# A new hand-written order on TensorE, VectorE and ScalarE in a top-k attention and MLP kernel: pacing by estimated engine times, a PSUM bank for the values, a shorter weight conversion, loads in order of need

## The chip, the cores and the metric

The kernel runs on one core of a Trainium2 chip. The metric is the device time of one execution in microseconds (us). Engines are named as the profile names them: PE is TensorE (PEld its weight loads), DVE is VectorE, ACT is ScalarE, POOL is GpSimd, SP is SyncE, whose queue issues the DMAs here. All numbers are float32, apart from the two MLP weights, which arrive as float64.

## What is computed

Attention with a top-32 mask, and on its output an MLP with a smooth ReLU:

```python
B, H, S, D = 8, 8, 576, 64
scores = q @ k.T / sqrt(D)                     # per batch and head: 576 x 576
kth    = the 32nd largest score of each row
attn   = softmax(where(scores >= kth, scores, -1e9))
x      = (attn @ v) as (B*S, H*D) = 4608 x 512
h      = x @ w_in                              # 512 x 2048
g      = where(h >= 1, h, where(h <= -1, 0, (h + 1)**2 / 4))
out    = g @ w_out                             # 2048 x 512
```

## The kernel before, in words

**Steps.** Rows of queries are taken in tiles of 128 (four whole tiles and a tail of 64 rows per batch). One *step* is one tile of queries for one pair of heads: 144 steps, numbered m = 0 to 143, 18 per batch. A step consists of these parts, each in a function of its own:

- `scores` (before: line 209): four matmuls (L221) into four PSUM tiles `sp`, each evicted by ACT to `s` (L224).
- `weights` (L229): on DVE. The row's larger and smaller halves are formed (`more` L238, `less` L256), four rounds of MAX8 and MATCH_REPLACE8 (L244, L251) find the 32nd largest; ACT computes the exponentials `e` (L248) from the row maximum, which POOL negates (`nmax`, L246); DVE applies the mask and sums (L271), POOL multiplies by the reciprocal (L279).
- `transpose_w` (L283): PE transposes `e` into `pw` and `pwt` (L290, L293), and ACT copies them to `wT` and `wTt`.
- `values` (L297): PE multiplies with the values into `po` (L305, L313), and ACT copies to `xT` (L318, L320).

`keys_of` (L170) and `queries_of` (L196) load and transpose the keys of a batch and the queries of a tile (`pk`, `pkt`, `pq`).

**MLP.** Tiles of 128 tokens are gathered in chunks, mostly of two tiles. `mlp` (L329) turns a chunk into a list of small pieces. `hidden(f)` makes 128 of the 2048 hidden channels: four matmuls into `ph` (L336), then ACT writes `r` and `g` from `ph` (L340, L342), and POOL finishes `g` in three operations (L343 to L345); there are two buffers of `r`. `final` makes the output of one tile in `py` (L353), two of the sixteen `f` at a time; after the last, ACT copies `py` to `y` (L357), which a DMA stores. A hidden piece of a two-tile chunk and a final piece cost 8 units each, a hidden piece of one tile 4; there are 4608 units in all.

**Weights.** The float64 weights come as pairs of 32-bit words in 64 pieces of 128 x 256 values. `weight_piece` (L78) makes float32 of them with integer operations: three DVE operations (L85, L86, L90), two on ACT (L92, L97), two on POOL (L93, L94), and one more on DVE (L99). They are converted inside `weights`, through the calls of `between()`, one piece at each of six places in a step, from step 0 on; four pieces come ahead of step 0. A piece of MLP work is placed only where the weights that it needs have been converted earlier in the program.

**PSUM.** There are eight banks: four under the tag "a", taken in turn by `sp`, `pk`, `pkt`, `pq`, `pw`, `pwt` and `po`; three for `ph`; one for `py`.

**The order.** On PE and DVE the instructions stand as the program issues them (`manual_schedule`, L411). On ACT, POOL and SP a scheduler chooses the order when the program is built. The loop (L445) issues for step m: `values(m-2)`, `scores(m+1)`, `weights(m)`, a share of the waiting MLP pieces, `transpose_w(m-1)`, the queries and keys that come next, and another share. `advance` (L401) places pieces up to an even share of what is left over the steps that are left. A chunk's pieces become available two steps after its last step: the first chunk at m = 5, the second at m = 9, the third at m = 17.

**After the loop**, a check that the 32nd value was found rightly (`excess`, L264) is reduced to one flag (L478 to L483); were it set, the program would run again with a slower, exact search. With these inputs it is not set.

Of the kernel before, what the change touches and what calls it, by code (L numbers as in the profile page):

```python
# [22 lines left out]
def kernel(  # L23
# [34 lines left out]
    nc.gpsimd.memset(half, 0.5)  # L58
    minus = const.tile([P, 1], F32, name="minus")
    nc.gpsimd.memset(minus, -1.0)  # L60
    w_in = const.tile([P, NK, DFF], F32, name="w_in")
    w_out = const.tile([P, NF, DM], F32, name="w_out")

# [12 lines left out]
    WC = 256  # L76

    def weight_piece(pool, dst, src):  # L78
        raw = pool.tile([P, 2 * WC], U32, name="raw", bufs=2)
        nc.sync.dma_start(out=raw, in_=src.bitcast(U32))  # L80
        words = raw.rearrange("p (n t) -> p n t", t=2)
        lo, hi = words[:, :, 0], words[:, :, 1]

        top = pool.tile([P, WC], U32, name="top", bufs=2)
        nc.vector.tensor_scalar(top, hi, 3, 0x3FFFFFFF, ALU.logical_shift_left, ALU.bitwise_and)  # L85
        nc.vector.scalar_tensor_tensor(out=top, in0=hi, scalar=0xC0000000, in1=top,  # L86
                                       op0=ALU.bitwise_and, op1=ALU.bitwise_or)

        unit = pool.tile([P, WC], U32, name="unit", bufs=2)
        nc.vector.tensor_scalar(unit, top, 0xFF800000, None, ALU.bitwise_and)  # L90
        low = pool.tile([P, WC], F32, name="low", bufs=2)
        nc.scalar.activation(low, lo, AF.Copy, scale=2.0 ** -52)  # L92
        nc.gpsimd.tensor_tensor(out=low, in0=low, in1=unit.bitcast(F32), op=ALU.mult)  # L93
        nc.gpsimd.tensor_tensor(out=low, in0=low, in1=top.bitcast(F32), op=ALU.add)  # L94

        size = pool.tile([P, WC], F32, name="size", bufs=2)
        nc.scalar.activation(size, hi.bitcast(F32), AF.Abs)  # L97
        yield
        nc.vector.scalar_tensor_tensor(out=dst, in0=size, scalar=1.125 * 2.0 ** -15, in1=low,  # L99
                                       op0=ALU.is_ge, op1=ALU.mult)  # L100

    def weight_pieces(pool):
# [19 lines left out]
    def run(ctx, paired):  # L122
# [47 lines left out]
        def keys_of(b):  # L170

            kT = stage.tile([P, NHP, S], F32, name="kT")
            v_in, v_tl = load_values(b)
            k_tl = stage.tile([TL, H, D], F32, name="k_tl", bufs=1)
            nc.sync.dma_start(out=k_tl, in_=k[b, :, SM:S, :].rearrange("h p d -> p h d"))
            for hp in range(NHP):
                k_in = stage.tile([P, NT, 2, D], F32, name="k_in")
                for j in range(2):
                    nc.sync.dma_start(out=k_in[:, :, j, :], in_=whole(k, b)[:, 2 * hp + j])
                pt = ps.tile([P, NT, P], F32, name="pk", tag="a", bufs=4)  # L180
                for c in range(NT):
                    nc.tensor.transpose(pt[:, c, :], k_in[:, c].rearrange("p j d -> p (j d)"), ident)
                for j in range(2):
                    d = slice(j * D, (j + 1) * D)
                    nc.scalar.copy(kT[d, hp, main(j)], pt[d].rearrange("p c n -> p (c n)"))
                if hp == 0:
                    pt = ps.tile([P, NHP, TL], F32, name="pkt", tag="a", bufs=4)
                    for h2 in range(NHP):
                        nc.tensor.transpose(pt[:, h2, :], k_tl[:, 2 * h2:2 * h2 + 2].rearrange("p j d -> p (j d)"),
                                            ident[0:TL, 0:TL])  # L190
                    for j in range(2):
                        d = slice(j * D, (j + 1) * D)
                        nc.scalar.copy(kT[d, :, tail(j)], pt[d])
                yield dict(kT=kT, v=v_in, v_tl=v_tl)

        def queries_of(q_in, t):  # L196
            n = P if t < NT else TL
# [99 lines left out]
        def values(st):  # L297
            t, hp, v_in, v_tl = st["t"], st["hp"], st["keys"]["v"], st["keys"]["v_tl"]
            wT, wTt = st["wT"], st["wTt"]
            po = ps.tile([P, P], F32, name="po", tag="a", bufs=4)  # L300
            if t < NT:
                for c in range(NT + 1):
                    for j in range(2):
                        h = 2 * hp + j
                        nc.tensor.matmul(po[j * D:(j + 1) * D], v_in[:, h, c, :] if c < NT else v_tl[0][:, h, :],  # L305
                                         wT[:, j, c, :] if c < NT else wTt, start=(c == 0), stop=(c == NT))
            else:
                for i in range(2):
                    cols = slice(i * TL, (i + 1) * TL)
                    for c in range(NT + 1):  # L310
                        for j in range(2):
                            h = 2 * (hp + i) + j
                            nc.tensor.matmul(po[j * D:(j + 1) * D, cols], v_in[:, h, c, :] if c < NT else v_tl[1][:, h, :],  # L313
                                             wT[:, i, c, j * TL:(j + 1) * TL] if c < NT else wTt[:, j * TL:(j + 1) * TL],
                                             start=(c == 0), stop=(c == NT))
            xT, col = st["xT"]
            if t < NT:
                nc.scalar.copy(xT[:, hp, col:col + P], po)  # L318
            else:
                nc.scalar.copy(xT[:, hp:hp + 2, col:col + TL], po.rearrange("p (i n) -> p i n", i=2))  # L320
# [7 lines left out]

        def mlp(xT, tiles, pool):  # L329
            cw = len(tiles) * P  # L330
            gs = []

            def hidden(f):
                ph = ps.tile([P, CW], F32, name="ph", tag="ph", bufs=3)[:, 0:cw]
                for kk in range(NK):
                    nc.tensor.matmul(ph, w_in[:, kk, f * P:(f + 1) * P], xT[:, kk, 0:cw],  # L336
                                     start=(kk == 0), stop=(kk == NK - 1))
# [10 lines left out]
            def final(i, f0, f1, pys={}):  # L348
# [4 lines left out]
                    nc.tensor.matmul(py, gs[f][:, i * P:(i + 1) * P], w_out[:, f, :],  # L353
                                     start=(f == 0), stop=(f == NF - 1))
                if f1 == NF:
                    y = pool.tile([P, DM], F32, name="y", bufs=2)
                    nc.scalar.copy(y, py)  # L357
                    for p0, p1, rows in rows_of(*tiles[i]):
                        nc.sync.dma_start(out=rows, in_=y[p0:p1])
# [38 lines left out]
                converted += 1  # L398
                next(pieces_left)

        def advance(amount):  # L401
            nonlocal spent, due
            due += amount
            while pending and pending[0][1] <= converted and due >= pending[0][0]:
                cost, _, work = pending.popleft()
                due -= cost
                spent += cost
                work()
            due = min(due, 8.0)

        order = tc.manual_schedule(engines={mybir.EngineType.PE, mybir.EngineType.DVE})  # L411
        order.__enter__()
        keys, xTs = {}, {}
        q_ins, qTs = {}, {}
# [3 lines left out]
                q_ins[rounds[i]] = load_queries(*rounds[i])  # L418

        fetch(0)  # L420
        for got in keys_of(0):
            keys[0] = got
        fetch(1)
        prep = None
        state = []

        def queries(m):
            if m < n and steps[m][0:2] not in qTs:
                r = steps[m][0:2]
                qTs[r] = queries_of(q_ins[r], r[1])  # L430
                fetch(rounds.index(r) + 2)

        def begin(m):
            b, t, hp, ch, col = steps[m]
# [4 lines left out]

        queries(0)  # L440
        begin(0)
        for _ in range(4):
            convert()
        next_keys = 1
        for m in range(n + 2):  # L445
            if 2 <= m:
                values(state[m - 2])
                state[m - 2] = None
                for ch in [c for c in range(len(chunks)) if ready[c] == m - 2]:
                    pending.extend(mlp(xTs[ch], chunks[ch], mlp_pool))  # L450
            share = (total - spent) / (n + 2 - m)
            if m + 1 < n:
                begin(m + 1)
            if m < n:
                weights(state[m], convert)
            advance(share / 2)
            if 1 <= m <= n:
                transpose_w(state[m - 1])
            queries(m + 2)
            if m < n and prep is None and next_keys < B and steps[m][0] == next_keys - 1 and steps[m][1] >= 1:  # L460
                prep = keys_of(next_keys)
            if prep is not None and m % 2 == 0:
                got = next(prep, None)
                if got is None:
                    prep, next_keys = None, next_keys + 1
                else:
                    keys[next_keys] = got
            advance(share / 2)
        while pending:
            advance(8.0)  # L470
        order.__exit__(None, None, None)

    with ExitStack() as inner:
        run(inner, True)
    flag = const.tile([1, 8], I32, name="flag")
    with tc.tile_pool(name="end", bufs=1) as end, tc.tile_pool(name="endps", bufs=1, space=PSUM) as endps:
        worst = end.tile([P, 8], F32, name="worst")
        nc.vector.max(out=worst, in_=excess)  # L478
        pt = endps.tile([1, P], F32, name="pt")
        nc.tensor.transpose(pt, worst[:, 0:1], ident)  # L480
        top = end.tile([1, 8], F32, name="top8")
        nc.vector.max(out=top, in_=pt)
        nc.vector.tensor_scalar(flag, top, 0.0, None, ALU.is_gt)  # L483
    again = nc.values_load(flag[0:1, 0:1], min_val=0, max_val=1)
    with tc.If(again > 0):
        with ExitStack() as inner:
# [28 lines left out]
```

## Time and profile before

| what | us |
|---|---|
| median of 3 runs | 1920.29 (1918.97 to 1921.25) |
| the profiled execution | 1915.05, its span 1913.0 |
| first conversion of a weight piece on DVE starts | 18.28 |
| DVE starts step 0, step 1, step 10, step 17, step 143 | 30.56, 51.95, 252.18, 333.16, 1845.01 |
| last `py` matmul ends, and `y` is issued to be stored | 1904.7, 1905.36 |
| the five steps on DVE from 291.59 to 344.85, each | 10.3 to 11.7 |
| mean of one DVE conversion operation, L85, L86, L90, L99 | 0.377, 0.557, 0.367, 0.44 |
| mean of one POOL operation on 128 x 256 values, L93, L94 | 0.788, 0.836 |

How to read it: a step on DVE begins with `more` (L238), so the starts of that line are the clock of the kernel. In a group of instructions the first number is the busy time, the second the mean of one in ns, then the idle time of the engine just before them, with what ended it. The trace records each float32 matmul as two, so that a hidden piece of a two-tile chunk shows as 8 records of 128x256. A row of the timeline gives start, length, engine, line, operation, tiles, how many, and in brackets the idle time ahead of it.

### The profile page before, as it was taken

Reading aid. Unit: us, or ns where it says so; the run is one execution under the profiler, and the core shown is the slowest. Engines: PE = TensorE matmul, PEld = TensorE weight load, DVE = VectorE, ACT = ScalarE, POOL = GpSimd, SP = SyncE. Lnnn points to the kernel's source line nnn. Section 1 sums busy time; section 2 is a strip of 40 time slices with the busy share of each in tenths; the row PEclk is TensorE's granted clock in tenths of the full one; section 3 lists DMA queues with packets and bytes.
Section 4 is the critical chain, followed back from the end, with each engine's and each line's share of the span. In section 5 each row is a group of like instructions: output and inputs, shape, how many; then the busy total and the mean of one; then the engine's idle time right before and its main releaser. Section 6 shows DMA issues by size and latency. Waiting matters only on the chain.

```text
span 1913.0 us, 32251 instructions
## 1 busy us (share of the span) xinstructions
PE 1679.1 (88%) x10129; PEld 1160.1 (61%) x10129; DVE 1625.4 (85%) x5011; ACT 977.1 (51%) x2429; POOL 1028.8 (54%) x1772
## 2 busy tenths in 40 slices
PE   2346478898999999998999999998999999998998
PEld 1234255656676685767575776666676667666565
DVE  5998989999999799999898898989987879879640
ACT  4345455546455564655454655555455555445432
POOL 3567572725454672818283674637274554553553
PEclk8667679899999999999999999999999999998999
DMA  6222210011010000110010000110010000000000
GB/s 173 80 78 77 77 28 17 26 30 24 9 40 20 23 18 23 32 36 12 16 38 23 21 12 24 40 27 12 23 31 25 11 12 11 10 12 7 6 7 14
DMA packets 107445, 57.75 MB, mean 30 GB/s; under 512 B 86272, under 2 KB 94464, under 8 KB 107264
## 3 DMA queue, kind: packets, MB, share of 16 engines
q1 hardware_dynamic: 107264, 55.59, 10.6%
q8 instruction: 82, 1.34, 0.3%
q14 instruction: 99, 0.81, 0.1%
HBM read 46.14 MB, written 9.44 MB: 29 GB/s over the span
## 4 chain that ended last, share of the span: by engine, by line
PE 53%; DVE 22%; POOL 13%; ACT 6%; issue 5%; DMA 1%; POOLq 0%; SPq 0%; DVEq 0%; ACTq 0%
PE py L353 24%; PE ph L336 11%; PE sp L221 6%; DVE tops L244 6%; PE po L305 5%; DVE more L251 5%; PE pw L290 4%; POOL g L345 4%; POOL r L344 3%; POOL e L279 2%; POOL r L343 2%; DVE e L271 2%; DVE more L238 2%; DVE seconds L259 2%; DVE less L256 1%
## 5 line engine op out<-in xcount | busy, mean ns | idle before, releaser
L353 PE MATMUL py<-w_out,g 128*128 128x512 f32 x1152 | 534.7, 607 | 41.7 <-DVE w_out L99 37.1
L336 PE MATMUL ph<-xT,w_in 128*128 128x256 f32 (+1 forms) x2816 | 553.3, 353 | 3.9 <-ACT g L342 2.8
L336 PEld LDWEIGHTS ph<-xT,w_in 128*128 128x128 f32 x2816 | 466.4, 197 | 83.0 <-issue 29.4
L244 DVE MAX8 tops<-more 128x8 f32<-128x288 f32 x1152 | 468.5, 448 | 5.0
L353 PEld LDWEIGHTS py<-w_out,g 128*128 128x128 f32 x1152 | 209.2, 191 | 286.4 <-issue 219.8
L251 DVE MATCH_REPLACE8 more<-tops,more 128x288 f32<-128x288 f32 x864 | 375.9, 443 | 0.0
L279 POOL TENSOR_SCALAR e<-e,rz 128x576 f32<-128x576 f32 x288 | 242.4, 850 | 130.9 <-DVE rz L277 104.9
L340 ACT ACTIVATE r<-ph,half 128x256 f32<-128x256 f32 (+1 forms) x352 | 153.9, 437 | 264.2 <-POOL g L345 135.2
L264 POOL TENSOR_TENSOR excess<-seconds,kth 128x2 f32<-128x2 f32 x144 | 39.2, 273 | 417.3 <-DVE kth L263 416.4
L271 DVE SCALAR_TENSOR_TENSOR e<-s,kth,e 128x576 f32<-128x576 f32 x288 | 242.4, 875 | 23.1 <-ACT e L248 6.6
L345 POOL TENSOR_TENSOR g<-r,g 128x256 f32<-128x256 f32 (+1 forms) x352 | 246.7, 701 | 24.0
L291 ACT COPY wT<-pw 128x512 f32<-128x512 f32 x288 | 155.5, 594 | 202.3 <-PE pw L290 202.3
L290 PE MATMUL pw<-ident,e 128*128 128x128 f32 x1152 | 161.5, 284 | 110.6 <-POOL e L279 105.9
L248 ACT ACTIVATE e<-s,nmax 128x576 f32<-128x576 f32 x288 | 213.1, 786 | 75.2 <-POOL nmax L246 74.4
L238 DVE TENSOR_TENSOR more<-s 128x576 f32<-128x576 f32 x144 | 130.4, 905 | 139.0 <-ACT s L224 138.6
L344 POOL TENSOR_TENSOR r<-r 128x256 f32<-128x256 f32 (+1 forms) x352 | 230.4, 655 | 26.1
L290 PEld LDWEIGHTS pw<-ident,e 128*128 128x128 f32 x1152 | 138.0, 146 | 162.5 <-POOL e L279 118.2
L221 PE MATMUL sp<-kT,qT 64*128 64x288 f32 x1024 | 196.5, 442 | 34.7 <-ACT xT L318 26.4
L224 ACT ACTIVATE s<-sp 128x288 f32<-128x288 f32 x576 | 197.9, 417 | 40.7 <-PE sp L221 36.8
L343 POOL TENSOR_SCALAR r<-r 128x256 f32<-128x256 f32 (+1 forms) x352 | 155.4, 441 | 93.5 <-ACT r L340 93.2
L305 PEld LDWEIGHTS po<-wT,v_in 128*64 128x64 f32 x2048 | 118.0, 140 | 74.8 <-issue 40.0
L221 PEld LDWEIGHTS sp<-kT,qT 64*128 64x128 f32 x1024 | 109.1, 189 | 84.6 <-ACT xT L318 39.4
(61 smaller groups left out, 1592.7 us busy)
## 6 DMA issues: line engine op xcount, KB each, us to landing
q_in<-in_q_dram SPq DMA_DIRECT2D x32, 256.0 KB, 3.0
v_in<-in_v_dram SPq DMA_DIRECT2D x8, 1024.0 KB, 5.8
k_in<-in_k_dram SPq DMA_DIRECT2D x64, 128.0 KB, 3.0
raw<-in_moe_w_in_dram SPq DMA_DIRECT2D x32, 256.0 KB, 2.7
raw<-in_moe_w_out_dram SPq DMA_DIRECT2D x32, 256.0 KB, 2.8
out_dram<-y SPq DMA_DIRECT2D x32, 256.0 KB, 2.3
v_tail<-in_v_dram SPq DMA_DIRECT2D x16, 64.0 KB, 2.5
k_tl<-in_k_dram SPq DMA_DIRECT2D x8, 128.0 KB, 3.2
```

The lines of the kernel that those rows point to most:

```text
L221: nc.tensor.matmul(o[:, a0 - c0:a1 - c0], qT[d, g, :], kT[d, g, k0:k0 + a1 - a0], start=True, stop=True)
L244: nc.vector.max(out=tops[:, i, r:r + 8], in_=src[:, i, :])
L248: nc.scalar.activation(e[:, i, :], s[:, i, :], AF.Exp, bias=nmax[:, i:i + 1])
L251: nc.vector.match_replace(out=rest[:, i, :], in_to_replace=tops[:, i, r:r + 8], in_values=src[:, i, :], imm_value=LOWEST)
L271: nc.vector.scalar_tensor_tensor(out=e[:, i, :], in0=s[:, i, :], scalar=last[:, i:i + 1], in1=e[:, i, :], op0=ALU.is_ge, op1=ALU.mult, acc ...
L279: nc.gpsimd.tensor_scalar(e[:, i, :], e[:, i, :], rz[:, i:i + 1], 1.0, ALU.mult, ALU.mult)
L290: nc.tensor.transpose(pt[:, c, :], w[:, i, main(i)][:, c * P:(c + 1) * P], ident)
L305: nc.tensor.matmul(po[j * D:(j + 1) * D], v_in[:, h, c, :] if c < NT else v_tl[0][:, h, :], wT[:, j, c, :] if c < NT else wTt, start=(c == ...
L336: nc.tensor.matmul(ph, w_in[:, kk, f * P:(f + 1) * P], xT[:, kk, 0:cw], start=(kk == 0), stop=(kk == NK - 1))
L344: nc.gpsimd.tensor_tensor(out=r, in0=r, in1=r, op=ALU.mult)
L345: nc.gpsimd.tensor_tensor(out=g[:, 0:cw], in0=r, in1=g[:, 0:cw], op=ALU.add)
L353: nc.tensor.matmul(py, gs[f][:, i * P:(i + 1) * P], w_out[:, f, :], start=(f == 0), stop=(f == NF - 1))
```

## The change

It has six parts. (1) PE's pacing: `advance` gets a second way to place a piece, when a running estimate of PE's time (`pe_time`) lies before an estimate of DVE's (`done`), and is called three times in a step instead of two; queries and keys are placed ahead of `transpose_w`. (2) ACT's order is the program's, as PE's and DVE's are; in it the exponentials of step m stand ahead of the copies of `wT` of step m-1. (3) `po` gets a bank of its own. For that, two hidden pieces share one bank: `ph` is a tile of [128, 2, 256] with two buffers instead of [128, 256] with three. (4) A weight piece takes three DVE operations (L87, L96, L98 of the new file) instead of four, one on POOL (L91, an int32 add) instead of two, and 7 or 8 pieces are converted in a step, after 7 ahead of step 0. (5) The values of a batch are loaded after its keys, the tail of the keys after the first pair of heads, and `raw` has three buffers. (6) The check of `excess` is made inside the loop, at m = 144, ahead of the last chunk's MLP; `y` has one buffer.

```diff
     def weight_piece(pool, dst, src):
-        raw = pool.tile([P, 2 * WC], U32, name="raw", bufs=2)
+        raw = pool.tile([P, 2 * WC], U32, name="raw", bufs=3)
...
-        top = pool.tile([P, WC], U32, name="top", bufs=2)
-        nc.vector.tensor_scalar(top, hi, 3, 0x3FFFFFFF, ALU.logical_shift_left, ALU.bitwise_and)
-        nc.vector.scalar_tensor_tensor(out=top, in0=hi, scalar=0xC0000000, in1=top,
-                                       op0=ALU.bitwise_and, op1=ALU.bitwise_or)
-        unit = pool.tile([P, WC], U32, name="unit", bufs=2)
-        nc.vector.tensor_scalar(unit, top, 0xFF800000, None, ALU.bitwise_and)
-        low = pool.tile([P, WC], F32, name="low", bufs=2)
-        nc.scalar.activation(low, lo, AF.Copy, scale=2.0 ** -52)
-        nc.gpsimd.tensor_tensor(out=low, in0=low, in1=unit.bitcast(F32), op=ALU.mult)
-        nc.gpsimd.tensor_tensor(out=low, in0=low, in1=top.bitcast(F32), op=ALU.add)
+        bits = pool.tile([P, WC], U32, name="bits", bufs=2)
+        nc.vector.tensor_scalar(bits, hi, 3, None, ALU.logical_shift_left)
+        units = pool.tile([P, WC], F32, name="units", bufs=2)
+        nc.scalar.activation(units, lo, AF.Identity, bias=two, scale=2.0 ** -51)
+        nc.gpsimd.tensor_tensor(out=bits.bitcast(I32), in0=bits.bitcast(I32), in1=units.bitcast(I32), op=ALU.add)
         size = pool.tile([P, WC], F32, name="size", bufs=2)
         nc.scalar.activation(size, hi.bitcast(F32), AF.Abs)
         yield
-        nc.vector.scalar_tensor_tensor(out=dst, in0=size, scalar=1.125 * 2.0 ** -15, in1=low,
+        nc.vector.scalar_tensor_tensor(out=bits, in0=hi, scalar=0x80000000, in1=bits,
+                                       op0=ALU.bitwise_and, op1=ALU.bitwise_or)
+        nc.vector.scalar_tensor_tensor(out=dst, in0=size, scalar=1.125 * 2.0 ** -15, in1=bits.bitcast(F32),
                                        op0=ALU.is_ge, op1=ALU.mult)
...
         def values(st):
-            po = ps.tile([P, P], F32, name="po", tag="a", bufs=4)
+            po = ps.tile([P, P], F32, name="po", tag="po")
...
             def hidden(f):
-                ph = ps.tile([P, CW], F32, name="ph", tag="ph", bufs=3)[:, 0:cw]
+                if f % 2 == 0:
+                    phs.append(ps.tile([P, 2, CW], F32, name="ph", tag="ph", bufs=2))
+                ph = phs[-1][:, f % 2, 0:cw]
...
-        def advance(amount):
+        K_TIME, PIECE_TIME, UNIT_TIME = 10.2, 1.2, 0.22
+        pe_time, dve_time, done = 8.0, 10.0, {}
+
+        def advance(amount, until=0.0):
             due += amount
-            while pending and pending[0][1] <= converted and due >= pending[0][0]:
+            while pending and pending[0][1] <= converted and (due >= pending[0][0] or
+                                                              pe_time + pending[0][0] * UNIT_TIME < until):
                 cost, _, work = pending.popleft()
-                due -= cost
+                due = max(due - cost, 0.0)
                 spent += cost
+                pe_time += cost * UNIT_TIME
                 work()
...
-        order = tc.manual_schedule(engines={mybir.EngineType.PE, mybir.EngineType.DVE})
+        order = tc.manual_schedule(engines={mybir.EngineType.PE, mybir.EngineType.DVE, mybir.EngineType.Activation})
...
             if m + 1 < n:
                 begin(m + 1)
-            if m < n:
-                weights(state[m], convert)
-            advance(share / 2)
-            if 1 <= m <= n:
-                transpose_w(state[m - 1])
+                pe_time += 1.15
+            advance(share / 4)
             queries(m + 2)
...
-            advance(share / 2)
+            advance(share / 4, done.get(m - 1, 0.0) + 2.5)
+            if m < n:
+                quota, before = (7 if m < 4 else 8), converted
+                ...
+                weights(state[m], between)
+                dve_time = max(dve_time, pe_time if m == 0 else 0.0) + K_TIME + PIECE_TIME * (converted - before)
+                done[m] = dve_time
+            if 1 <= m <= n:
+                pe_time = max(pe_time, done[m - 1] + 2.0) + 1.0
+                transpose_w(state[m - 1])
+            if m == n and paired:
+                judge(ps, att)
+            advance(share / 2, pe_time + 1.5)
```

`between` of the new loop spreads the 7 or 8 pieces evenly over the six places of a step. `judge` holds the operations that stood after the loop: MAX8 over `excess`, a transpose on PE, MAX8 and a comparison on DVE. In `keys_of`, `load_values` moves behind the last pair of heads, and the load of `k_tl` behind the first loads of `k_in`. Batch 0 takes its first step's queries and scores after its first pair of heads, and the other three pairs after that, each with the conversion of one weight piece.

## The prediction

> **What bounds the kernel now.** I read the page's busy times and slices first, then a table of stretches, the waits, and the timeline of single steps.
>
> ```profile
> PE 1679.1 (88%) x10129; PEld 1160.1 (61%) x10129; DVE 1625.4 (85%) x5011; ACT 977.1 (51%) x2429; POOL 1028.8 (54%) x1772
> PE   2346478898999999998999999998999999998998
> DVE  5998989999999799999898898989987879879640
> PEclk8667679899999999999999999999999999998999
> ...
> 0.00:48.00 48.00, 11.18 (x48) 8.09 (x48) 25.29 (x69) 19.72 (x46) 17.88 (x32) 0.82 0.66 172
> 96.00:144.00 48.00, 20.09 (x133) 15.82 (x133) 43.99 (x122) 22.89 (x62) 32.89 (x51) 0.68 0.26 76
> 574.00:765.00 191.00, 187.69 (x1118) 126.79 (x1117) 171.05 (x543) 104.10 (x258) 101.03 (x181) 1.00 0.08 21
> ```
>
> The columns of the last three are the stretch, its length, the busy time of PE, PEld, DVE, ACT and POOL, and the granted clock. There are two stages. Until about 250 us DVE is full (attention and conversion), and PE works 20 of 48 us at a clock of 0.68. From there on PE is full (187.7 of 191) and DVE waits for it:
>
> ```profile
> DVE more L238 <- ACT s L224: 138.6, 68, 8.5
> PE sp L221 <- ACT xT L318: 26.4, 24, 5.2
> PE sp L221 <- ACT xT L320: 5.7, 6, 1.7
> PE pk L182 <- ACT wT L291: 11.8, 7, 3.8
> ACT r L340 <- POOL g L345: 135.2, 132, 3.4
> ```
>
> So from step 17 (333.2 us, when the third chunk opens) PE's own time decides; before it, DVE's. PE's time there is regular: with 32 units of MLP a step without a wait takes 10.5 us from one `pw` to the next (494.3 to 504.7), with 40 units 12.2 (691.4 to 703.6); eight records of 128x256, 8 units, take 1.78. That makes 0.222 us a unit and 3.41 us of attention a step. The 127 steps from 17 on hold 4352 units; all over, 433 + 966 = 1399 us. They take 1572 to the last matmul, 173 more: 46 for keys, queries and tail steps, 48 in `sp`, 12 in `pk`, some 33 where no MLP work is ready and PE waits for DVE, 20 in slow clock after such waits, the rest small.
>
> **The change part by part.** One profiled execution took 1915.05, 0.3% under the median of 1920.29; I sum against 1915 and add the sum to the median.
>
> *Placement by estimate, and faster conversion.* I counted the units of each step in the compiled order of both kernels. From step 34 to the end every step holds the same number; only the first three chunks move (88 units at m = 5 against 40, the rest up to three steps earlier). Both start the third chunk at step 17, with the same 256 units done. So this part can only win the time by which DVE reaches step 17 sooner. Old: 333.2. New: a piece costs DVE 0.377 + 0.557 + 0.444 = 1.38 instead of 1.74 (the rows of L85, L86, L99; the added operations have the forms of L85 and L86). A step without pieces is 21.4 less 6 x 1.74 = 10.9 early on, 10.4 later. Seven pieces ahead of step 0 wait for `raw`, whose fourth load stands behind 3.1 MB of keys, queries, values and three pieces; at the 172 GB/s of the first stretch that is 18 us and more, so step 0 starts near 29 (between 25, were the loads no limit, and 33). Steps 0 to 7 with 57 pieces: 8 x 10.9 + 57 x 1.38 = 166, less 5 since POOL works less beside DVE: 161. Steps 8 to 16: 98. Sum 288, 45 earlier. The int32 add on POOL has no row; the nearest are L94's 0.84 and, as an upper end, twice that. I take 0.84: eight are 7 of a 21 us step. At 1.7 each double place stalls DVE by 0.9, 18 us in all.
>
> *ACT in program order.* Against those 45 stands m = 5: all sixteen hidden pieces of chunk 0 are issued ahead of step 5's exponentials, and the conversion's ACT work stands behind these. POOL needs 0.36 + 0.46 + 0.51 per 128-wide piece, 21 us for sixteen, and PE in pairs (below) 25. DVE reaches the first piece that it can't finish about 6.5 us into step 5, and gets it near 32: a stall of 26 (0, if the pieces are done by then; 30 with a slow clock). Elsewhere in the first steps I put 5. Step 17 then starts at 319: **-14**. Later, exponentials ahead of the `wT` copies let DVE have `e` about 1 us earlier, which is worth nothing while PE decides.
>
> *A bank for `po`.* The fourth `sp` takes the bank that `po` had, so PE waits for the `xT` copy. After 333 us, 58 of the 102 score groups of whole tiles take 1.24 us, and the mean is 1.71. In the compiled order the new `sp` waits for no ACT instruction: **-48** (from the 32 of the two wait rows up to 50 with the tail steps). Keys ahead of `pw` find free banks: **-12**.
>
> *Two hidden pieces in one bank.* The compiled order shows that the odd piece's first matmul waits for ACT's `g` of the even piece of the same tile; before, a piece waited for the `g` of three pieces earlier. Of 176 pairs 16 come before step 17 and 8 in the last chunk; of the rest 84 follow each other directly. 28 have values and scores between (2.4 us, enough), 29 `pw` (1.15), 11 queries or keys. What a direct pair costs is read here:
>
> ```profile
> 704.60 3.62 PE L336 MATMUL ph<-xT,w_in 128*128 128x256 f32 x16
> 705.03 0.47 ACT L340 ACTIVATE r<-ph,half 128x256 f32<-128x256 f32 x1 [2.04 <-POOL g L345]
> 705.40 0.47 ACT L342 ACTIVATE g<-ph,minus 128x256 f32<-128x256 f32 x1
> 705.76 1.07 ACT L291 COPY wT<-pw 128x512 f32<-128x512 f32 x2
> 706.70 0.30 ACT L294 COPY wTt<-pwt 128x128 f32<-128x128 f32 x1
> 706.86 1.48 ACT L248 ACTIVATE e<-s,nmax 128x576 f32<-128x576 f32 x2
> 708.20 0.50 ACT L340 ACTIVATE r<-ph,half 128x256 f32<-128x256 f32 x1
> 708.56 0.51 ACT L342 ACTIVATE g<-ph,minus 128x256 f32<-128x256 f32 x1
> ```
>
> The first of two pieces ended at 706.38, its `g` at 709.07: PE, which went on at once into another bank, would have stood for 2.7 us. A piece after `pw` meets ACT busy with copies and exponentials. The two pieces before them, which began at 700.06 behind scores alone, give 1.2 (half done at 701.84, `g` ended at 702.99, and 0.06 from a `g` to a waiting PE at 648.79). I take 2.2 for the 22 wide pairs right after `pw`, 1.2 for the other 34 wide ones, 1.05 for 28 narrow ones (`r` and `g` 0.63 at 1876.35, and about 0.4 to and from ACT): 48 + 41 + 29 = 118. Split pairs: 29 x 0.15 + 11 x 0.7 = 12; the last chunk 2. **+132** (67 if only the two reads of 0.8 us count; 215 if all wide ones cost 2.7). What covered this was the third bank: PE's waits for `ph` were 2.8 us in all. Where PE now comes later to a stretch without MLP work, it waits less for DVE: **-12** of the 33.
>
> *Clock.* After 1.47 us of waiting at 1389.5 the next 24 records took 7.13 us, against 5.33 elsewhere; after 1.32 at 803.8 nothing was slow. So short waits sometimes cost 1.8 us. There will be more, though spread: **+5** (-10 to +90).
>
> The Trainium skill, "TensorE: Matmul & The Clock Gate", section "Why this matters for your kernels", has the clock fall only after gaps of more than about 3 us. By that this term would be nothing and the sum 5 less; the row at 1389.5 speaks against it, and the row decides. Its page "PSUM — Partial Sum Buffer", section "PSUM bank collisions raise a hardware error", says to guard PSUM by bank, not by address, which speaks against the shared bank: by it the wait inside a pair must stand, where guarding by address would take the 132 away. No row here has two pieces in one bank.
>
> *With one answer.* `y` with one buffer: copies are 14 us and more apart, the store is issued 0.02 us after the copy at the end and lands in 2.3: nothing, unless SP is stuck behind a load (it waits up to 26 us for `pk`). Values after keys: issued some eight steps ahead of use, and step 0's values at 53 us in the old trace: nothing. Two more ACT operand reads and one memset: nothing, ACT is 51% busy. `judge` ahead of the last chunk: PE and DVE save the 0.8 us after the last copy: **-1**; its wait for DVE is covered by POOL's 1.8 us of scaling.
>
> Sum: -14 - 48 - 12 + 132 - 12 + 5 - 1 = +50, that is 1965 for this execution and **1970** for the median.
>
> **The rivals.** *A pair costs little* (faster): the odd piece waits, but the evictions come at once. What speaks for it: ACT is idle half the time; against: the rows above. At 0.6 us per direct pair the +132 become +52 and the time 1890. It decides below a mean of 1.0 us over the 84 pairs. *The gaps drop the clock* (slower still): if every second of some 60 steps with hidden pieces runs one group at half clock, 30 x 1.8 us more, or with POOL's queue in each gap, the time is 2025. For it: 1302 and 1773 us, where groups of 16 and 24 records took 5.3 and 7.2 us instead of 3.7 and 5.4, after waits of 3.8 and 5.2; against: PE stays above 80% busy. *The parts cancel* (no change): gaps near 1.0.
>
> **How the numbers follow.** Forecast 55% (its own range 1938 to 2005), clock or queue 19%, cheap pairs 21%, cancelled 5%. Less than 0.2% (4 us) can't be told from no change. The range leaves out the better half of the cheap pairs and the worse half of the slow clock, a tenth each: 1888 to 2040.
>
> **What would show it.** Right: a row of PE `ph` waiting for ACT `g` of 100 us or more; `sp` waiting for `xT` gone; step 17 near 319 with one long DVE stall in step 5; steps with hidden pieces near 13 us and those with `py` alone near 10.5 to 12.3. Wrong: a `ph` wait under 80 us, step 17 before 300, or DVE full to the end.

## The result, and the profile after

The changed kernel takes 2004.94 us (median of 4 runs, 2002.96 to 2005.43), against 1920.77 for the kernel before on the same chip: 1.0437 times as long, with a 95% interval of 1.0419 to 1.0455. The forecast was 1970 with a range of 1888 to 2040. The direction and its main cause held; the loss of 84 us was sized as 50.

The profiled execution took 2005.43 us with a span of 2003.6, so it stands 90.4 above the profiled execution before. Its busy times and slices:

```profile
PE 1675.9 (84%) x10129; PEld 1139.5 (57%) x10129; DVE 1572.0 (78%) x4947; ACT 992.1 (50%) x2429; POOL 946.4 (47%) x1709
PE   3226586898999899989999899989998998987987
DVE  5884879798989778888988788898886788769640
PEclk9858798999999999999999999999999999998999
```

PE has the same 10129 instructions and about the same busy time (1679.1 before), yet many of its nines have gone to eights, and so have DVE's: in more slices than before, neither of the two is full. The table of stretches of the same kernel (stretch, length, busy time of PE, PEld, DVE, ACT, POOL, granted clock, DMA share, GB/s) shows where:

```profile
96.00:144.00 48.00, 10.99 (x63) 7.64 (x64) 38.09 (x106) 22.63 (x53) 15.26 (x23) 0.61 0.27 85
144.00:191.00 47.00, 27.82 (x177) 21.46 (x176) 20.32 (x57) 20.04 (x57) 25.18 (x60) 0.83 0.14 44
574.00:765.00 191.00, 179.36 (x1132) 125.67 (x1132) 161.95 (x512) 102.94 (x259) 111.21 (x200) 0.99 0.09 22
```

From 144 to 191 us DVE, the engine that sets the early stage, works 20 of 47 us. From 574 to 765, where PE sets the time, it works 179.4 of 191 at a clock of 0.99; before it was 187.7 at 1.00. So the clock isn't what is lost; the waits of the changed kernel are (engine, tile, line, releaser: total us, times, longest):

```profile
PE ph L340 <- ACT g L346: 125.3, 115, 2.3
PE po L307 <- ACT wT L293: 125.2, 28, 19.9
DVE e L273 <- ACT e L250: 247.7, 73, 16.8
DVE bits L96 <- POOL bits L91: 49.2, 13, 25.1
```

The first row was 2.8 us before, the second 5.4; PE's waits of `sp` for the `xT` copy, 32 us before, are gone. The timeline of the changed kernel shows one pair of hidden pieces in its bank (start, length, engine, line, operation, tiles, shape, count, and in brackets the idle time ahead):

```profile
707.74 1.44 ACT L250 ACTIVATE e<-s,nmax 128x576 f32<-128x576 f32 x2
707.79 1.89 PE L340 MATMUL ph<-xT,w_in 128*128 128x256 f32 x8
709.07 1.07 ACT L293 COPY wT<-pw 128x512 f32<-128x512 f32 x2
710.01 0.29 ACT L296 COPY wTt<-pwt 128x128 f32<-128x128 f32 x1
710.17 0.51 ACT L344 ACTIVATE r<-ph,half 128x256 f32<-128x256 f32 x1
710.54 0.51 ACT L346 ACTIVATE g<-ph,minus 128x256 f32<-128x256 f32 x1
711.10 1.99 PE L340 MATMUL ph<-xT,w_in 128*128 128x256 f32 x8 [1.41 <-ACT g L346]
```

The even piece is done at 709.68. ACT is busy with exponentials and the copies of `wT` and `wTt` until 710.2, reads the bank until 711.05, and PE begins the odd piece at 711.10 after standing for 1.41 us. The same rows show a second loss: the `wT` copies stand behind the exponentials, since ACT now keeps the program's order.

Two kinds of numbers carry the rest. *Step 17* is the start of `more` in that step on DVE, when the third chunk opens: 333.2 us before, 345.1 after, so 12 of the 90 us were lost ahead of it. For the time from there to the last matmul I gave each PE record of the timeline the time from the end of the record ahead of it to its own end, and added by tile:

| PE time after step 17, us | before | after | two banks, below | free ACT, below | once per pair and free ACT, below |
|---|---|---|---|---|---|
| `ph` records + idle ahead | 501.2 + 2.8 | 520.7 + 111.9 | 491.7 + 23.5 | 526.4 + 121.0 | 486.9 + 0.2 |
| `po` | 168.7 + 2.1 | 177.0 + 24.1 | 180.9 + 23.7 | 174.0 + 9.2 | 173.0 + 9.2 |
| `sp` | 191.1 + 30.3 | 163.2 + 0 | 162.8 + 0 | 162.9 + 0 | 162.9 + 0 |
| `pw`, `pwt` | 143.9 | 141.3 | 141.9 | 136.4 | 139.5 |
| `pk`, `pkt` | 28.2 | 13.4 | 13.5 | 14.0 | 14.3 |
| `py` | 486.4 | 484.8 | 484.7 | 485.2 | 485.4 |

`ph` gained 128.6 us, `po` 30.3; `sp` lost 58.2, the keys 14.8, `pw` 2.6, `py` 1.6: 82 in sum, against 80 measured between step 17 and the last matmul (1572.5 before, 1652.6 after; records across the border fall out, 5.3 us of `ph` among them in the column of two banks).

### The profile page after: what moved, and what is told of

Same layout as the page of the kernel before. It is cut to its first block, busy times and chain, and to the rows that moved or that the text cites. A ratio compares the mean times of both kernels' runs of the same rounds, so it can differ in the third digit from the quotient of the medians.

```text
span 2003.6 us, 32150 instructions
## 1 busy us (share of the span) xinstructions
PE 1675.9 (84%) x10129; PEld 1139.5 (57%) x10129; DVE 1572.0 (78%) x4947; ACT 992.1 (50%) x2429; POOL 946.4 (47%) x1709
## 4 chain that ended last, share of the span: by engine, by line
PE 65%; DVE 14%; ACT 10%; issue 6%; POOL 3%; DMA 1%; SPq 0%; ACTq 0%; DVEq 0%; POOLq 0%
PE py L357 24%; PE ph L340 20%; PE sp L223 8%; PE po L307 7%; PE pw L292 3%; DVE tops L246 3%; ACT r L344 3%; DVE more L253 3%; ACT e L250 2%; ACT g L346 2%; DVE e L273 2%; ACT wT L293 1%; DVE bits L96 1%; POOL e L281 1%; DMA raw<-in_moe_w_in_dram 1%
## 5 line engine op out<-in xcount | busy, mean ns | idle before, releaser
L340 PE MATMUL ph<-xT,w_in 128*128 128x256 f32 (+1 forms) x2816 | 569.0, 352 | 126.0 <-ACT g L346 125.3
L340 PEld LDWEIGHTS ph<-xT,w_in 128*128 128x128 f32 x2816 | 452.9, 193 | 232.8 <-ACT g L346 166.7
L357 PE MATMUL py<-w_out,g 128*128 128x512 f32 x1152 | 532.3, 603 | 16.6 <-DVE w_out L98 13.4
L281 POOL TENSOR_SCALAR e<-e,rz 128x576 f32<-128x576 f32 x288 | 258.8, 907 | 249.8 <-DVE rz L279 226.1
L307 PE MATMUL po<-wT,v_in 128*64 128x128 f32 x2048 | 167.1, 298 | 126.2 <-ACT wT L293 125.2
L307 PEld LDWEIGHTS po<-wT,v_in 128*64 128x64 f32 x2048 | 127.2, 147 | 200.7 <-ACT wT L293 142.3
L348 POOL TENSOR_TENSOR r<-r 128x256 f32<-128x256 f32 (+1 forms) x352 | 215.7, 613 | 27.6
L292 PE MATMUL pw<-ident,e 128*128 128x128 f32 x1152 | 154.2, 277 | 38.1 <-POOL e L281 18.6
L347 POOL TENSOR_SCALAR r<-r 128x256 f32<-128x256 f32 (+1 forms) x352 | 135.9, 387 | 95.8 <-ACT r L344 94.9
L223 PE MATMUL sp<-kT,qT 64*128 64x288 f32 x1024 | 175.5, 460 | 5.9 <-ACT kT L185 4.8
L320 ACT COPY xT<-po 128x128 f32<-128x128 f32 x128 | 34.1, 266 | 266.2 <-PE po L307 265.9
```

What stands on the lines that cost most here:

```text
L223: nc.tensor.matmul(o[:, a0 - c0:a1 - c0], qT[d, g, :], kT[d, g, k0:k0 + a1 - a0], start=True, stop=True)
L281: nc.gpsimd.tensor_scalar(e[:, i, :], e[:, i, :], rz[:, i:i + 1], 1.0, ALU.mult, ALU.mult)
L292: nc.tensor.transpose(pt[:, c, :], w[:, i, main(i)][:, c * P:(c + 1) * P], ident)
L348: nc.gpsimd.tensor_tensor(out=r, in0=r, in1=r, op=ALU.mult)
```

## The experiments

The theory: PE stands inside each pair because ACT must have read the even piece before PE may write the odd one, and this costs some 125 us whatever ACT's order is; apart from it, ACT's fixed order costs the early stage through the stall in step 5. The rival: ACT's fixed order, or the placement, makes all evictions late, and the shared bank only shows it. In some of these kernels the lines stand two higher or lower than in the changed kernel.

**Two banks of one piece each.**

```diff
-                if f % 2 == 0:
-                    phs.append(ps.tile([P, 2, CW], F32, name="ph", tag="ph", bufs=2))
-                ph = phs[-1][:, f % 2, 0:cw]
+                ph = ps.tile([P, CW], F32, name="ph", tag="ph", bufs=2)[:, 0:cw]
```

> The changed kernel, but each hidden piece has a bank of its own (two in all, where the changed kernel has two banks of two pieces each); po keeps its own bank. Theory (the shared bank makes the odd piece wait for the even one's eviction): the 125 us in which PE's ph waits for ACT's g fall below 40, and the time falls from 2005 to about 1895 (1875 to 1925). Rival (ScalarE in program order, or the placement, makes the evictions late; the bank only shows it): two banks wait as much as the shared ones, the ph wait stays above 80 us and the time above 1970.

Measured: 1885.31 us (1884.60 to 1885.71), ratio to before 0.983 (0.981 to 0.985). Its waits:

```profile
PE po L307 <- ACT wT L293: 125.3, 28, 19.8
PE ph L338 <- ACT g L344: 27.1, 23, 2.3
```

The `ph` wait falls by 98 us and the time by 120, with ACT's order and the placement left as they were: the rival falls. The `po` row stays at 125.3, so it has another cause. With one bank per piece, a piece waits only for the eviction of the piece two earlier; the same two banks, each half used, are enough to do better than the kernel before.

**Three banks, and `po` among the scores again.** The edit of the run above with `bufs=3`, and

```diff
-            po = ps.tile([P, P], F32, name="po", tag="po")
+            po = ps.tile([P, P], F32, name="po", tag="a", bufs=4)
```

> The changed kernel with the banks of the kernel before: three banks of one hidden piece each, po again among the four banks of the scores. Theory: the ph wait is below 10 us, and the wait of sp for the xT copy comes back with 25 to 50 us, so the time is about 1930 (1905 to 1945), 20 to 50 above the run with two single banks and po apart. Rival (a bank for po is worth nothing): the same time as the run with two single banks, or less.

Measured: 1916.98 us (1915.36 to 1920.79), ratio 0.9996 (0.9987 to 1.0006), 31.7 above the run with two banks.

```profile
PE sp L223 <- ACT xT L320: 26.5, 19, 2.5
PE ph L338 <- ACT g L344: 6.9, 5, 2.2
```

The `sp` wait is back and the `ph` wait gone. A bank for `po` is worth 32 us here although its price, a third bank for `ph`, costs 20 of waits. And with the old banks the whole of the rest of the change (order, pace, conversion, loads) is worth nothing: 0.9996.

**ACT's order left to the scheduler.**

```diff
-        order = tc.manual_schedule(engines={mybir.EngineType.PE, mybir.EngineType.DVE, mybir.EngineType.Activation})
+        order = tc.manual_schedule(engines={mybir.EngineType.PE, mybir.EngineType.DVE})
```

> The changed kernel with ScalarE's order left to the scheduler again; banks, placement, conversion and loads as changed. Theory (two causes apart: the bank costs PE 125 us whatever ScalarE's order is, the order costs the start of the third chunk some 25 us through the stall in step 5): the ph wait stays between 90 and 140 us, step 5 has no stall above 10 us, step 17 starts near 318 and the time is about 1980 (1965 to 1995). Rival (the fixed order is what makes the evictions late): the ph wait falls below 60 and the time below 1940.

Measured: 1963.23 us (1962.16 to 1966.25), 42 less than the changed kernel; ratio to before 1.0239 (1.0222 to 1.0256).

```profile
PE ph L340 <- ACT g L346: 146.2, 117, 4.2
PE po L307 <- ACT wT L293: 16.1, 26, 2.3
```

The `ph` wait stays, even larger than I had allowed (146.2 against at most 140): a free order doesn't help a pair. Step 5 lasts 27.4 us in place of 48.0, step 17 starts at 310.8 in place of 345.1. That is 34 of the 42 us (I had expected step 17 near 318, and the time is 2 us under my range); the 109 us of `po` waiting that go are partly in those 34 and partly after them (18 by the table above, of which `ph` takes back 15).

**The banks of the change in the kernel before.** Both bank edits of the change and nothing else.

> The kernel before with the change of banks alone: po apart, two hidden pieces in one bank. Theory: ph waits of 100 to 140 us appear, sp's wait for xT goes, and the time is about 1995 (1970 to 2015), since 125 us come in and some 45 go. Rival (the bank hurts only under the fixed order of ScalarE or the new placement): ph waits below 40 us and a time of 1870 to 1900.

Measured: 1995.31 us (1992.66 to 1996.00), ratio 1.040 (1.038 to 1.042).

```profile
PE ph L338 <- ACT g L344: 145.6, 118, 4.1
```

The two bank edits by themselves cost 78 of the 84 us that the whole change costs. All else that it does adds up to 6 with these banks, and to nothing with the old ones.

**Both undone: two banks of one piece, ACT free.**

> The changed kernel with two banks of one hidden piece each and ScalarE's order left to the scheduler. Theory (the two losses are separate): the 120 us of the bank and the 42 us of ScalarE's order add up, so the third chunk opens near 304 us and the time is about 1846 (1835 to 1862), below the kernel before. Rival (with the bank mended, the start of the third chunk is hidden by something else): no better than the two single banks alone, 1875 to 1890.

Measured: 1864.39 us (1859.80 to 1866.00), ratio 0.972 (0.970 to 0.974); step 17 at 305.0. The order was worth 21 us more, not 42. The early stage gained 28.8, as expected, but then `ph` waits rose from 23.5 to 34.4 us and `pq` got 6.5 of them: it seems that under a free order ACT comes to the evictions somewhat later, and that two single banks feel it. So my sum of the two was 18 too hopeful; both parts of the theory stand, but they aren't wholly separate.

**Without the running estimate.** `until` is not given any more, so that pieces go by their share alone.

```diff
-            advance(share / 4, done.get(m - 1, 0.0) + 2.5)
+            advance(share / 4)
...
-            advance(share / 2, pe_time + 1.5)
+            advance(share / 2)
```

> The changed kernel, but the MLP units go by their share of the rest alone: the running estimate no longer calls more of them. In the compiled order step m = 5 gets 6 hidden pieces ahead of the conversion and the exponentials in place of 16, and the same 256 units stand before the third chunk. Theory (the stall in step 5 is the sixteen pieces in ScalarE's fixed order): step 5 lasts under 38 us in place of 48, some of it comes back as 3 to 5 us in each of steps 6 and 7, the third chunk opens between 334 and 341 and the time is 1990 to 2002. Rival (the stall comes from the order of conversion and exponentials alone): step 5 stays at 46 to 50 us and the time at 2005.

Measured: 1985.95 us (1985.25 to 1986.53), 19 less than the changed kernel. Step 5 lasts 34.0 us, steps 6 and 7 together 60.3 (47.0 with the estimate); step 17 starts at 341.4. The stall in step 5 is indeed the sixteen pieces, and most of it moves on to the next two steps. But 16 of the 19 us come after step 17, where I had expected nothing: steps 17 to 33 take 187.0 us in place of 203.3, and from 34 on both are alike. The time is just under my range. PE's `ph` wait in those steps, without the estimate and then in the changed kernel:

```profile
PE ph L340 <- ACT g L346: 5.9, 6, 1.7
```

```profile
PE ph L340 <- ACT g L346: 17.2, 15, 1.5
```

The difference of the two rows is 11 of the 16 us. In the compiled order the estimate puts four pieces instead of three ahead of the first `pw` of a chunk. After that, two pieces stand in each place in both kernels. With three ahead, each later place holds the end of one pair and the start of the next, and the score, value or `pw` work between the places covers the eviction. With four ahead, each place holds one whole pair, and PE waits inside it. The number of direct pairs after step 16 is 92 with the estimate and 81 without, and as many waits of `ph` begin right behind another `ph` record in the two traces. One piece more or less at the start of a chunk decides for the whole chunk.

**A pair evicted once.** The two pieces stay in one bank, but `r` and `g` are read out once for both, after the second, and POOL's three operations take both at once.

```diff
+                if f % 2 == 0:
+                    return
+                both = phs[-1][:, :, 0:cw]
-                r = pool.tile([P, CW], F32, name="r", bufs=2)[:, 0:cw]
-                nc.scalar.activation(r, ph, AF.Relu, bias=half, scale=0.5)
-                g = pool.tile([P, CW], F32, name="g", bufs=NF)
-                nc.scalar.activation(g[:, 0:cw], ph, AF.Relu, bias=minus, scale=1.0)
+                r = pool.tile([P, 2, CW], F32, name="r", bufs=2)[:, :, 0:cw]
+                nc.scalar.activation(r, both, AF.Relu, bias=half, scale=0.5)
+                gp = pool.tile([P, 2, CW], F32, name="g", bufs=NF // 2)
+                g = gp[:, :, 0:cw]
+                nc.scalar.activation(g, both, AF.Relu, bias=minus, scale=1.0)
...
-                gs.append(g)
+                gs.extend([gp[:, 0], gp[:, 1]])
```

> The changed kernel with the two hidden pieces still in one bank, but r and g are taken from the bank once for both pieces, after the second, and GpSimd works on both at once. ScalarE's order stays fixed. Theory (what costs is the read that stands between the two halves of a bank, not the sharing): the ph wait falls below 30 us, the time to about 1880 (1860 to 1900). Rival (two pieces in a bank cost PE by themselves, or the longer evictions come too late): ph waits above 80 us, time above 1950.

Measured: 1850.32 us (1849.13 to 1852.84), ratio 0.964 (0.963 to 0.966). That is 10 us below my range. No row of `ph` waiting for `g` is left among its waits. So it is the read between the two halves that costs, and not that two pieces share a bank. It is also 35 us better than two single banks: ACT's busy time falls from 986.9 to 927.5 us and POOL's from 969.5 to 858.2, since one operation over both pieces takes 0.61 us where two took 0.44 each, and DVE's wait for the exponentials falls from 130.3 to 56.4. How the 35 us divide over these isn't shown.

**The same with ACT free.**

> As the run before it, and ScalarE's order left to the scheduler. Theory: another 35 to 42 us less, about 1842 (1825 to 1862), the third chunk near 304. Rival: no better than the fixed order, 1875 or more, since larger instructions on ScalarE delay the exponentials.

Measured: 1803.11 us (1802.21 to 1803.62), ratio 0.940 (0.938 to 0.941), the best kernel of the study and better than both kernels of the case. A free order is worth 47 us here, more than the 35 to 42 that I had expected. Step 17 starts at 299.3. Its stretch from 574 to 765, in the columns of above:

```profile
574.00:765.00 191.00, 191.00 (x1237) 136.54 (x1235) 180.48 (x553) 104.68 (x233) 104.22 (x138) 1.00 0.09 24
```

PE doesn't wait at all in it: 191.00 of 191, with 1237 records where the changed kernel got 1132 done.

**Conversion and loads alone.** The kernel before with `weight_piece` and `keys_of` of the changed kernel (and `y` with one buffer, to make room).

> The kernel before with two parts of the change: the three-operation conversion (raw with three buffers, y with one to make room) and the loads in order of need. Placement, ScalarE's order and banks stay as before. Theory (DVE sets the early stage and nothing after it changes): a piece costs DVE about 1.47 us in place of 1.74, the first step starts some 2 us earlier, ten steps with six pieces gain 1.6 us each, so the third chunk opens near 315 (308 to 322) and the time is about 1900 (1890 to 1910). Rival (the dearer last operation and the wait for GpSimd's integer add eat the gain): the third chunk opens after 326, time 1910 or more.

Measured: 1889.51 us (1885.80 to 1890.45), ratio 0.984 (0.982 to 0.986). Step 17 starts at 306.9, 26.3 earlier than before: and the whole gain at the end is 29.8, so what the early stage gains goes through to the end. Both are a little better than my ranges. How much of the gain is the conversion and how much the loads wasn't tested.

**The pair evicted once in the kernel before.** `po` apart and the edit of the pair evicted once; nothing else of the change.

> The kernel before with banks alone changed, and in the other way: po apart, two hidden pieces in one bank, evicted once for both after the second. Conversion, loads, placement and ScalarE's order stay as before. Theory: sp's 32 us of waiting for xT go, no ph wait above 10 us comes, and ScalarE's and GpSimd's shorter work takes more of the rest: about 1860 (1840 to 1880). Rival (70 of the 176 pairs are split by other PE work, so that the first half's eviction comes too late for its readers): 1900 or more.

Measured: 1839.05 us (1838.47 to 1843.49), ratio 0.959 (0.957 to 0.961), 1 us below my range. The same two banks that cost 78 us with a read inside each pair gain 80 with one read after it.

**The best kernel without the estimate.** ACT free, pairs evicted once, `until` not given.

> The changed kernel with pairs evicted once, ScalarE's order left to the scheduler, and the running estimate no longer calling units. Theory (with no wait inside a pair, where the units of the first three chunks stand doesn't matter, since 256 units stand before the third chunk either way): the same time as with the estimate, 1803 within 6. Rival (the estimate fills TensorE's idle time in the early stage): 1812 or more.

Measured: 1806.93 us (1806.28 to 1807.79), ratio 0.942 (0.940 to 0.943), against 0.940 (0.938 to 0.941) with it. Step 17 starts at 301.4 against 299.3. Without waits inside pairs, where the first chunks' pieces stand is worth 4 us.

## Why the prediction was right or wrong

**The pairs, +132: right, and nearly the size.** The table gives 128.6 for `ph`. It came together differently: 111.0 us of waiting in 99 waits after step 17, 1.12 each, where I had 1.40 for a direct pair. The other 19.5 us are longer `ph` records, which I hadn't priced, so that the total lies so near is partly luck. Eight records behind a wait span 1.99 us (711.10), where I had 1.78 for eight; 99 times the difference is 21, an estimate that fits. Whether PE starts slowly after a wait or the modelled ends of records show it, no run here tells. Undoing it gave 120 back at ACT's fixed order, so the mechanism is shown. (The upper end of 215 that I gave needs the 11 pairs with queries or keys between at 2.7 us as well; with the direct ones alone the sum is 195.)

**`po`'s bank, -48, and the keys, -12: right.** `sp` lost 58.2, the keys 14.8. For the keys the two parts overlap: their time, 28.2 us before, is 17.5 with the banks alone and 13.8 with all but the banks. The gaps inside the score groups, which I read from group lengths rather than from the 32 us of the wait rows, were the better measure.

**Less waiting for DVE, -12: mostly missed.** `pw` and `pwt` lost 2.6 us, since ACT's order delays DVE itself (`e` waits for its exponentials for 236 us after step 17); with a free order they lose 7.5.

**The order of ACT after step 17, taken as worth nothing: wrong by some 18 us of `po`.** I noticed that exponentials ahead of the `wT` copies bring `e` about 1 us sooner, and left it there, because PE decides. The same order holds the `wT` copies back, and PE's `po` waits for these: 22 us more of waits and 8 of longer records, 30.3 in the table. A free order returns 18 of them, and these are shown to be its price; what the other 12 come from is open. I priced the side of the swap that comes sooner and not the one that comes later. What a free order saves in all from step 17 to the last matmul depends on the banks: 8 us in the changed kernel, where `ph` takes back 15; 24 with pairs evicted once; with two single banks it costs 3.

**The early stage, -14: wrong, it was +12.** The kernels of the study split it, by the start of step 17:

| kernel | step 17 | step before it in this list |
|---|---|---|
| before | 333.2 | |
| conversion and loads alone | 306.9 | -26.3 |
| and placement and bank for `po`, two banks, ACT free | 305.0 | -1.9 |
| and ACT's fixed order | 333.8 | +28.8 |
| and pairs in one bank (the changed kernel) | 345.1 | +11.3 |

I had 31 for ACT's order, 26 of it as the stall in step 5. The order cost 28.8, and the stall was where and as long as said; the timeline of DVE in the changed kernel:

```profile
175.13 1.00 DVE L96 SCALAR_TENSOR_TENSOR bits<-raw,bits 128x256 uint32<-128x256 uint32 x1 [25.07 <-POOL bits L91]
```

What failed is "Sum 288, 45 earlier". With ACT free and two banks it is 305, 28 earlier. The start (29.9 against 29) and steps 8 to 16 (97.6 against 98) were right; steps 0 to 7 took 177.4 us where I had 166 less 5. In them DVE waits 10.2 us for `bits` from POOL and 4.3 for `raw`, for which I had 5 in all and only under ACT's fixed order. And the 0.444 for the last operation of a piece (L98) was a duration from another neighbourhood: with POOL idle it takes 0.42 us (22 of 22 in the changed kernel), but mostly it meets a POOL operation, 36 times of 42 the new conversion's integer add, and then it takes 0.75 to 0.87 (40 of 42). L87 and L96 came cheaper than their terms, so that a piece's three operations took DVE 1.43 us in these eight steps against my 1.38, 3 us in all; most of the miss is the waits. The pair's bank, 11 us here, I had counted only inside step 5; in the kernel before the banks alone put step 17 at 343.8, 10.6 later.

**The clock, +5: in sum not seen.** From step 17 to the end the granted clock is 0.99 (345 to 1998 us), before it was 0.98 (333 to 1905). But a short wait can be followed by a slow clock. PE stood for 1.82 us up to 657.44, for a `g`, and right behind this the clock was at half:

```profile
654.40:657.80 3.40, 1.58 (x14) 1.39 (x13) 2.63 (x7) 2.98 (x8) 1.30 (x4) 1.00 0.13 30
657.80:661.20 3.40, 3.07 (x16) 2.78 (x14) 3.37 (x14) 0.85 (x3) 3.15 (x8) 0.51 0.02 5
```

The wait at 1389.5 before is of this kind (0.50 from 1392.3 to 1395.7 us), so the row was read rightly; what was wrong is that more waits would make more of it. The Trainium skill, "TensorE: Matmul & The Clock Gate", section "Why this matters for your kernels", warns of PE's idle gaps of over about 3 us; none of the 115 waits of `ph` is longer than 2.3, so the trace doesn't agree with that as a lower limit.

**PSUM guarded by bank.** I weighed the rule of the Trainium skill, "PSUM — Partial Sum Buffer", section "PSUM bank collisions raise a hardware error", to guard PSUM by bank: by it the wait inside a pair had to stand, and it stood, 115 times. The wait is in the compiled program; what the chip would do without it no run shows. The run with one eviction shows the other half: a bank may hold two pieces at no cost, if nobody reads until both are written.

**The rivals.** Cheap pairs would have needed less than 1.0 us for each of the 84; the waits alone were 1.12, the longer records come on top. The cancelling parts fall with it. Stretches at half clock there are, but no more than before, and ACT stands waiting for POOL in 14 of the 99 waits, for 7 of their 111 us; that the time lies nearer to that rival's 2025 than to 1970 comes from the early stage and the `po` waits.

The terms together, on the profiled executions: forecast -14 before step 17 and +64 after it; measured +12 and +80, and 1.4 less behind the last matmul.

## What to carry to other kernels

Two accumulation groups in one PSUM bank are free as long as the readers come once, after both; with a reader between them every pair costs the whole way through the reading engine's queue (here 1.2 us, 92 times where the two follow each other directly), and the placement decides how often. When an engine's order is changed, price what moves back as well as what moves up: here the exponentials moved up and the copies that PE waits for moved back. A part that gains (the shorter conversion with its loads, -1.6%; a bank for the values, 32 us) can be hidden whole by another beside it, so test the parts alone before the sum.

## What the runs showed of the hardware

That a DVE operation's duration depends on what POOL does at that moment was larger than I had expected. The timeline of the kernel with conversion and loads alone:

```profile
72.94 0.41 DVE L96 SCALAR_TENSOR_TENSOR bits<-raw,bits 128x256 uint32<-128x256 uint32 x1
73.16 0.77 POOL L91 TENSOR_TENSOR bits<-bits,units 128x256 int32<-128x256 int32 x1 [2.21 <-DVE bits L87]
73.45 0.77 DVE L98 SCALAR_TENSOR_TENSOR w_in<-size,bits 128x256 f32<-128x256 f32 x1
```

and one of the changed kernel, in which POOL has no operation at the time:

```profile
96.64 0.42 DVE L96 SCALAR_TENSOR_TENSOR bits<-raw,bits 128x256 uint32<-128x256 uint32 x1
97.16 0.42 DVE L98 SCALAR_TENSOR_TENSOR w_in<-size,bits 128x256 f32<-128x256 f32 x1
```

The same operation takes 0.77 beside POOL's add and 0.42 alone. In the first case POOL's add ends at 73.93 and DVE's operation 0.29 later, as if it did most of its work after POOL had finished. The Trainium skill, "SBUF — State Buffer", section "SBUF: two separate sides", says that a DVE operation with two SBUF inputs and a POOL operation that reads SBUF hold a shared port in turn, each for a whole instruction, and that the one that comes second blocks. The rows agree: in the changed kernel 40 of the 42 L98 that meet a POOL operation began after it, and each ended 0.27 to 0.28 us after that operation's end, also the six beside the scaling of `e` (L281). The two that began first took 0.42 and 0.43. Six L96 beside L281 took 0.42; five of them began 0.07 to 0.09 us ahead of it, one with it. In a sum of durations, the row to take is one with the same neighbour, and with the same one of the two first.
